# Retention attention with a gated product: where twelve tiles of g are kept, where one product stands, and how the last tile ends

## The chip, the cores and the metric

One NeuronCore of one Trainium2 chip runs the whole program. The metric is the time of one execution on the device in microseconds (us), lower is better. Names of engines: PE is the matrix engine (TensorE), PEld its weight loads, DVE the vector engine, ACT the scalar engine, POOL GpSimd, SP the engine that issues the DMAs (SPq is its queue). A line number with an L is a line of the kernel before, and, in the profile of the kernel after, a line of that one.

## The reference, cut to what matters

Four batches, eight heads, 768 tokens, 64 columns per head. A recurrent attention with one decay per head is followed by a product, a silu and a second product.

```python
gamma = 1.0 - 2.0 ** (-5.0 - np.arange(H))
state = 0
for t in range(S):
    state = gamma * state + k[:, :, t]^T v[:, :, t]        # per batch and head, 64x64
    y[:, :, t] = scale * q[:, :, t] @ state
x = y.transpose(0, 2, 1, 3).reshape(B * S, H * D)           # 3072 x 512
h = x @ w_in                                                # 512 -> 2048
g = h * (1 / (1 + exp(-h)))
return g @ w_out                                            # 2048 -> 512
```

All values are float32, and the kernel computes each product of float32 matrices from parts, so that one product of a tile takes several matmuls.

## The kernel before, in words

**Tiles.** The 768 tokens are cut in six chunks c of 128. A chunk of one batch is a *unit* (c, b), 24 in all, numbered 4c + b. For a unit, PE transposes k and q (the tiles kp, qp; L476 in one form, L485 in a form with 64-row pieces), computes scores within the chunk and the sums for the state (sc, L504 and L514), and y from scores and state (L562). DVE and ACT copy and scale in between (L423, L477, L490, L522, L530, L534, L609), and split x in the parts xt (L633, L636, L639). Such a piece of attention work on PE is called a *visit*. In one form a visit is cut in two halves: the first makes the transposes of unit m and y of unit m − 2, the second the scores of unit m − 1.

**First product.** product_in(c, f) multiplies the four units of chunk c (512 columns of xt) with slice f of 16 of w_in: twelve matmuls of 128x512 (L734), eight into the PSUM tile ha and four into hb. Then close_steps evacuates: ACT copies ha to a tile g (L744), DVE subtracts hb (L749), ACT applies the silu (L754). The tile g lies in the pool hpool, tag "hs", three buffers. put_g stores it to a DRAM tile g_dram[c, f] by a DMA on SP's queue (L757 to L760), one or more products later. (c, f) below means this product.

**Weights.** A slice of w_in is loaded by load_w (three DMAs on SP, L186 and L188), converted (L205 to L224) and split in three parts by split_steps (ACT L121, DVE L124, ACT L127, DVE L129) into a slot of the pool wpool: w0 to w11 and a fourfold slot wq. The slots w4 to w11 hold the k, q and v of the units 0 to 7 first (L161), until those are used up.

**Second product.** For every chunk the g are read back from DRAM (L773), split (L805, L807, L808) and multiplied with w_out: twelve matmuls per (c, f) and four batches into accumulators oa and ob (L1088). In the last chunk the last two slices f are done batch by batch (L1102), and each batch's result is put together and stored: ACT copies ob (L1116), DVE combines with oa (L1121), SP stores (L1124). For the last batch the matmuls into oa go in two halves of 256 columns, and so do the combine and the store.

**Order.** PE's order is written out by hand from end to end. That of SP, DVE, ACT and POOL is by hand only in the head, up to early_order.close() (L976); behind that a scheduler places their instructions, by data and buffers, with hints (issue_after, queue) that put one behind another. The head begins with matmuls on a zero tile (narrow: 128x32, fill: 128x512 and 128x256), which compute nothing that is used; narrow(39), fill(2), narrow(39) stand ahead of the transposes of unit 0 (L858 to L861). Behind the head comes product (1, 0), then, by L980, the first half of visit 10, and then the list steps (L982 to L990): (1,1), (1,2), (0,3), (1,3), (0,4), (1,4), then (0,5), (1,5), (2,0), and so on. Behind each of the first ones the next half visit follows (`behind`, L998). A DMA on SP takes one of eight semaphores in turn, and so waits for the landing of the one eight before.

Of the kernel before, what the change touches and what calls it, by code (L numbers as in the profile page):

```python
# [34 lines left out]
def kernel(  # L35
# [107 lines left out]
    FAR = 3 * B + 2  # L143
    ROWS = range(2 * B + 2, FAR - 1)
    LATER = 4 * B + 2
    early = {}

    def load(name, n):
        if n >= len(units):
# [24 lines left out]
    def load_w(i):  # L174
        if i >= 2 * NF:
            return
        if wide:
            t = stage.tile([128, 2 * DM], U32, tag="wf", name=f"wf_{i}")
            w_in, w_out, n = moe_w_in.bitcast(U32), moe_w_out.bitcast(U32), 256
        else:  # L180
            t = stage.tile([128, DM], FP32, tag="wf", name=f"wf_{i}")
            w_in, w_out, n = moe_w_in, moe_w_out, 128
        if i < NF:
            to = t.rearrange("p (i o f) -> o p i f", o=2, f=n)
            src = w_in[:, ts(i, n)].rearrange("(i o p) f -> o p i f", o=2, p=128)
            nc.sync.dma_start(out=to[0], in_=src[0])  # L186
            for j in range(2):
                nc.sync.dma_start(out=to[1, ts(j, D)], in_=src[1, ts(1 - j, D)])  # L188
        else:
            nc.sync.dma_start(out=t, in_=w_out[ts(i - NF, 128), :])  # L190
        staged[i] = t
# [128 lines left out]
    def narrow(out, n):  # L320

        for _ in range(n):
            nc.tensor.matmul(out[:, :32], lhsT=zero, rhs=zero[:, :32], start=True, stop=True,
                             skip_group_check=True)
# [404 lines left out]
    def multiply(c, f):  # L729
# [6 lines left out]
                                 stop=kk == KIN - 1 and i != 0)  # L736
        return ha, hb

    def close_in(*of):
        list(close_steps(*of))  # L740

    def close_steps(c, f, ha, hb):
        hs = hpool.tile([128, NT], FP32, tag="hs", name=f"g_{c}_{f}")
        copied[:] = [nc.scalar.activation(out=hs, in_=ha, func=AF.Copy, scale=ONE_E).ins]  # L744
        with queue(copied[0]):
            while behind_copy:
                behind_copy.pop(0)()
        yield
        taken_out[:] = [nc.vector.tensor_tensor(out=hs, in0=hs, in1=hb, op=ALU.subtract).ins]  # L749
        with queue(taken_out[0]):  # L750
            while behind_next:
                behind_next.pop(0)()
        yield
        nc.scalar.activation(out=hs, in_=hs, func=AF.Silu)  # L754
        pending.append((c, f, hs))

    def put_g(keep):  # L757
        while len(pending) > keep:
            c, f, g = pending.pop(0)
            stored[:] = [nc.sync.dma_start(out=g_dram[c, f], in_=g).ins]  # L760


    order = [(c, f) for c in range(NC) for f in range(NF)]
# [92 lines left out]
    K, Q = scale_k, scale_q  # L856

    idle[:] = [banks("y", "idle")[:, 0]]  # L858
    narrow(idle[0], 39)
    fill(idle[0], 2)  # L860
    narrow(idle[0], 39)  # L861
    T(0), K(0)
    nc.scalar.activation(out=token, in_=lgc[:1, :1], func=AF.Silu)
    SC(0), A(0), Q(0), A(0), A(0)
# [112 lines left out]
    written[0] = False  # L977

    half_visits = (x for m in range(EARLY + 2, 3 * B + 1) for x in chain(halves(m), (None,)))
    next(half_visits)  # L980

    half = NF // 2  # L982
    pairs = [(1, 1), (1, 2), (0, 3), (1, 3), (0, 4), (1, 4)]
# [12 lines left out]
    takes += [(4, f) for f in (0, 3, 7, 11, 14)]  # L996
    takes += [(5, f) for f in (2, 5, 8)]
    behind = {x: lambda: next(half_visits) for x in pairs[:-1]}  # L998
    behind[pairs[-1]] = lambda: [visit(3 * B + 1), behind_next.append(end_w)]
    at = ([(1, NF - 1)] + [(2, f) for f in range(NF - 7, NF - 2, 2)] +  # L1000
          [(c, 4 * i + 1) for c in range(3, NC - 1) for i in range(B)])
# [17 lines left out]
        turns_at[far[m] + 1], joins_at[far[m] + 3] = m, m  # L1019
    scales_at = {far[m] + 2: m for m in range(LATER - 1, len(units))}  # L1020
    scales_at[steps.index((0, NF - 2))] = FAR
    loads_at = {first_far + 4: [("k", FAR + 1), ("q", FAR + 1)], far[FAR] + 1: [("q", FAR + 2)]}
    for n, (c, f) in enumerate(steps):
        if n in scales_at:
            behind_next.append(lambda m=scales_at[n]: scale_k(m))
        if n in joins_at:
            behind_copy.insert(0, lambda m=joins_at[n]: [join_t(name, m) for name in "qk"])
        if n in parts:
            behind_next.append(lambda m=parts[n]: part_t(m, taken_out[0]))
        patient[0] = steps.index((3, 0)) <= n < max(turns_at) + 2  # L1030
        product_in(c, f)
        put_g(1)
        store_w()
        if (c, f) in takes:
            take_w(taken_out[0], n < len(pairs + three) or c == NC - 1)
        behind.get((c, f), lambda: None)()
        if n in turns_at:
            turn_t(turns_at[n])
            if turns_at[n] >= LATER:
                with tc.issue_after(turned_by[0]):  # L1040
                    load("k", turns_at[n] + 1), load("q", turns_at[n] + 1)
        if turns_at.get(n - 1, 0) >= LATER:
            with tc.issue_after(stored[0]):
                load("v", turns_at[n - 1] + 1)
        if turns_at.get(n - 2, 0) >= LATER:
            with tc.issue_after(stored[0]):
                while waiting:
                    load_w(waiting.pop(0))
        for name, m in loads_at.get(n, ()):
            load(name, m)  # L1050
        if c == NC - 1:
            if f == 0:
                for i in range(W_READ):
                    get_w(i)
            if f < NF - 4:
                w_out(f, True)
            if f >= NF - 6:
                if f == NF - 6:
                    for n in range(G_AHEAD):
                        get(n)  # L1060
                if f >= NF - S_AHEAD:
                    with tc.issue_after(taken_out[0]):
                        split(f - NF + S_AHEAD)
    put_g(0)

    for c in range(NC):
        acc = []
        for b in range(B):
            if b < 2:
                u = banks("sy"[b], f"o{b}_{c}")  # L1070
                acc.append([u[:, i] for i in range(2)])
            else:
                acc.append([turn(f"oa{b}_{c}"), turn(f"ob{b}_{c}") if b == 2 else
                            banks("q", f"ob{b}_{c}", 1)[:, 0]])
        early_f = NF if c < NC - 1 else NF - 2
        for f in range(NF):
            n = c * NF + f
            split(n + S_AHEAD)
            if n < 4:
                w_out(NF - 4 + n)  # L1080
            t = ready[n]
            if f >= early_f:
                continue
            for b in range(B):
                gh, glo, gm = (t[:, i, ts(b, C)] for i in range(3))
                oa, ob = acc[b]
                for o, g, i in (oa, gh, 0), (oa, glo, 1), (ob, gm, 2):
                    nc.tensor.matmul(o, lhsT=g, rhs=wo[f][:, i, :], start=f == 0 and i != 1,  # L1088
                                     stop=f == NF - 1 and i != 0)

        for b in range(B if early_f < NF else 0):
            oa, ob = acc[b]
            ends = [(ob, (2,), slice(None))]
            if b < B - 1:
                ends.append((oa, (0, 1), slice(None)))
            else:
                ends += [(oa, (0, 1), slice(i * DM // 2, (i + 1) * DM // 2))
                         for i in range(2)]
            for o, parts, cols in ends:
                for f in range(early_f, NF):  # L1100
                    for i in parts:
                        nc.tensor.matmul(o[:, cols], lhsT=ready[c * NF + f][:, i, ts(b, C)],  # L1102
                                         rhs=wo[f][:, i, cols], start=False,
                                         stop=f == NF - 1 and i != 0,
                                         skip_group_check=cols.start == DM // 2)
        for b in range(B):
            oa, ob = acc[b]
            o = one.tile([128, DM], FP32, tag=("kt", "qt")[b % 2], name=f"o_{c}_{b}",
                         bufs=(2, 3)[b % 2])
            rows = ds(b * S + c * C, C)  # L1110
            if c < NC - 1:
                nc.scalar.activation(out=o, in_=oa, func=AF.Copy, scale=ONE_E)  # L1112
                nc.vector.tensor_tensor(out=o, in0=o, in1=ob, op=ALU.subtract)
                nc.sync.dma_start(out=out[rows, :], in_=o)
                continue
            nc.scalar.copy(out=o, in_=ob)  # L1116

            n = 2 if b == B - 1 else 1
            for i in range(n):
                cols = ts(i, DM // n)  # L1120
                nc.vector.scalar_tensor_tensor(out=o[:, cols], in0=oa[:, cols], scalar=ONE_E,  # L1121
                                               in1=o[:, cols], op0=ALU.mult,
                                               op1=ALU.subtract)
                nc.sync.dma_start(out=out[rows, cols], in_=o[:, cols])  # L1124


# [28 lines left out]
```

## Time and profile before

| what | value |
|---|---|
| timed runs | 612.46, 613.16, 614.77 us, median 613.16 |
| the profiled execution: its span, first to last instruction | 612.56 us (612.6 on the page) |
| its own time | the span; the median of the timed runs lies 0.6 us above it |
| PE busy in it | 600.9 us, 98% of the span |
| DVE, ACT, POOL busy | 397.1, 324.5 and 32.9 us |
| DMA moved | 108.9 MB, mean 178 GB/s |
| last matmul to the end | 608.8 to 612.6 us |
| granted clock of PE in the page's rows | 1.00 |

How to read it: the page lists busy time per engine, the chain that ended last (followed back from the last instruction, at each step to what released it), and groups of instructions with mean times. Answers of the trace add waits (what ended an engine's idle time), windows (busy time by stretches), and a timeline, where a line has a start in us, a time in us, the engine, the line, the operation with its tiles (out<-in), and in brackets the engine's idle time before it with what ended it. Ends of matmuls are modelled.

### The profile page before, as it was taken

How to read it: one execution, taken by the hardware profiler on the slowest of the kernel's cores; microseconds unless marked ns; L12 is line 12 of the kernel's file. 1: busy time of each engine (PE TensorE's matmuls, PEld its weight loads, DVE VectorE, ACT ScalarE, POOL GpSimd, SP SyncE). 2: the span in 40 equal slices, each digit the busy share in tenths (PEclk: the TensorE clock that was granted, in tenths of full speed). 3: DMA queues.
4: the chain of work that ended last, by engine and by line, in shares of the span. 5: the costliest groups of instructions: out<-in, count | busy, mean ns of one | idle time of the engine just before them, and what ended most of it. 6: DMA issues, size and time to landing. Idle time of an engine off the chain costs nothing.

```text
span 612.6 us, 13713 instructions
## 1 busy us (share of the span) xinstructions
PE 600.9 (98%) x5509; PEld 495.9 (81%) x5509; DVE 397.1 (65%) x672; ACT 324.5 (53%) x598; POOL 32.9 (5%) x89
## 2 busy tenths in 40 slices
PE   8898999999999999999999999999999999999997
PEld 6686788888888888888888888888888888888886
DVE  4797898678886676766689774635545463645631
ACT  7688678678676667676698632212221322313211
POOL 3000020100021111210000000000000000000000
PEclk9999999999999999999999999999999999999999
DMA  9999976586799699998777542623524433433301
GB/s 195 209 199 231 258 214 203 160 254 188 258 231 233 154 263 263 258 291 255 248 249 267 169 138 69 206 69 106 169 72 136 137 110 97 152 123 99 107 1 69
DMA packets 144336, 108.90 MB, mean 178 GB/s; under 512 B 101137, under 2 KB 109585, under 8 KB 144273
## 3 DMA queue, kind: packets, MB, share of 16 engines
q1 hardware_dynamic: 144272, 108.03, 62.3%
q8 instruction: 43, 0.70, 0.5%
q14 instruction: 21, 0.16, 0.1%
HBM read 66.06 MB, written 36.70 MB: 168 GB/s over the span
## 4 chain that ended last, share of the span: by engine, by line
PE 92%; DMA 3%; SPq 2%; DVE 2%; issue 1%; ACT 0%; DVEq 0%
PE ha L734 28%; PE o L1088 21%; PE oa L1088 14%; PE hb L734 14%; PE ob L1088 7%; PE y L562 3%; DMA qf<-in_q_dram 2%; PE sc L504 1%; SPq L166 1%; PE sc L514 1%; DMA kqv<-in_v_dram 1%; SPq L188 1%; PE o L1102 0%; PE oa L1102 0%; PE kp L485 0%
## 5 line engine op out<-in xcount | busy, mean ns | idle before, releaser
L734 PE MATMUL ha<-xt,wi 128*128 128x512 f32 x768 | 193.0, 393 | 0.0
L734 PEld LDWEIGHTS ha<-xt,wi 128*128 128x128 f32 x768 | 142.4, 188 | 30.5 <-DVE xt L636 0.2
L1088 PE MATMUL o<-wo,gs 128*128 128x512 f32 x564 | 143.1, 389 | 0.0
L805 ACT ACTIVATE gs<-gr 128x512 fp32r<-128x512 f32 x96 | 53.2, 621 | 139.0 <-issue 138.0
L1088 PEld LDWEIGHTS o<-wo,gs 128*128 128x128 f32 x564 | 105.9, 188 | 22.0
L807 DVE TENSOR_TENSOR gs<-gr,gs 128x512 fp32r<-128x512 f32 x96 | 62.1, 684 | 94.2 <-ACT gs L805 94.2
L1088 PE MATMUL oa<-wo,gs 128*128 128x512 f32 x376 | 115.7, 389 | 0.0
L749 DVE TENSOR_TENSOR g<-g,hb 128x512 f32<-128x512 f32 x96 | 65.7, 684 | 57.6 <-ACT g L744 42.6
L734 PE MATMUL hb<-xt,wi 128*128 128x512 f32 x384 | 102.7, 389 | 0.0
L734 PEld LDWEIGHTS hb<-xt,wi 128*128 128x128 f32 x384 | 72.1, 188 | 15.1
L1088 PEld LDWEIGHTS oa<-wo,gs 128*128 128x128 f32 x376 | 70.5, 188 | 14.6
L754 ACT ACTIVATE g<-g 128x512 f32<-128x512 f32 x96 | 60.3, 629 | 37.7 <-DVE g L749 37.6
L1088 PE MATMUL ob<-wo,gs 128*128 128x512 f32 x188 | 73.1, 389 | 0.0
L744 ACT ACTIVATE g<-ha 128x512 f32<-128x512 f32 x96 | 56.7, 591 | 28.6 <-PE ha L734 19.8
L808 DVE SCALAR_TENSOR_TENSOR gs<-gs 128x512 fp32r<-128x512 f32 x96 | 62.0, 683 | 0.1
L1088 PEld LDWEIGHTS ob<-wo,gs 128*128 128x128 f32 x188 | 35.3, 188 | 7.4
L205 ACT ACTIVATE ca<-wf 128x512 f32<-128x512 f32 x32 | 21.6, 675 | 6.6 <-DVE cs L218 4.0
L522 DVE TENSOR_TENSOR am<-sc,decay 128x512 f32<-128x512 f32 x24 | 16.5, 687 | 11.4 <-PE sc L514 11.4
L1112 ACT ACTIVATE o<-o 128x512 f32<-128x512 f32 x10 | 6.0, 598 | 33.4 <-PE o L1088 33.0
L218 DVE SCALAR_TENSOR_TENSOR cs<-ca,cs 128x512 uint32<-128x512 uint32 x32 | 22.7, 710 | 0.9
L639 DVE SCALAR_TENSOR_TENSOR xt<-xt 128x512 fp32r<-128x512 f32 x28 | 19.9, 715 | 0.7
L562 PE MATMUL y<-qt,mid 64*64 64x64 f32 x376 | 19.4, 220 | 0.4 <-issue 0.4
(122 smaller groups left out, 562.2 us busy)
## 6 DMA issues: line engine op xcount, KB each, us to landing
gd<-g SPq DMA_DIRECT2D x96, 256.0 KB, 3.7
gr<-gd SPq DMA_DIRECT2D x96, 256.0 KB, 2.7
wf<-in_moe_w_out_dram SPq DMA_DIRECT2D x16, 512.0 KB, 4.7
out_dram<-o SPq DMA_DIRECT2D x23, 256.0 KB, 2.1
wf<-in_moe_w_in_dram SPq DMA_DIRECT2D x16, 256.0 KB, 4.6
wf<-in_moe_w_in_dram SPq DMA_DIRECT2D x32, 128.0 KB, 4.1
kf<-in_k_dram SPq DMA_DIRECT2D x16, 256.0 KB, 4.1
qf<-in_q_dram SPq DMA_DIRECT2D x16, 256.0 KB, 4.1
```

What stands on the lines that cost most here:

```text
L205: top = nc.scalar.activation(out=a.bitcast(FP32), in_=hi.bitcast(FP32), func=AF.Abs, scale=2.0 ** -3).ins
L218: nc.vector.scalar_tensor_tensor(out=s, in0=a, scalar=3, in1=s, op0=ALU.logical_shift_left, op1=ALU.bitwise_xor)
L562: i = nc.tensor.matmul(to[ts(e, D), o, a, :], lhsT=lhsT, rhs=rhs, start=key not in started, stop=True, skip_group_check=True).ins
L639: nc.vector.scalar_tensor_tensor(out=x[2], in0=x[1].bitcast(FP32), scalar=-1.0 / EPS, in1=x[0].bitcast(FP32), op0=ALU.mult, op1=ALU.add)
L734: nc.tensor.matmul(hb if i == 2 else ha, lhsT=w_sb[f][:, i, ts(kk, 128)], rhs=xt[c][:, i, kk, :], start=kk == 0 and i != 1, stop=kk == KIN ...
L744: copied[:] = [nc.scalar.activation(out=hs, in_=ha, func=AF.Copy, scale=ONE_E).ins]
L749: taken_out[:] = [nc.vector.tensor_tensor(out=hs, in0=hs, in1=hb, op=ALU.subtract).ins]
L754: nc.scalar.activation(out=hs, in_=hs, func=AF.Silu)
L805: nc.scalar.activation(out=t[:, 0, :], in_=g, func=AF.Copy, scale=HALF)
L807: nc.vector.tensor_tensor(out=t[:, 1, :], in0=g, in1=high, op=ALU.subtract)
L808: nc.vector.scalar_tensor_tensor(out=t[:, 2, :], in0=t[:, 1, :].bitcast(FP32), scalar=-1.0 / EPS, in1=high, op0=ALU.mult, op1=ALU.add)
L1088: nc.tensor.matmul(o, lhsT=g, rhs=wo[f][:, i, :], start=f == 0 and i != 1, stop=f == NF - 1 and i != 0)
```

## The change

It has four parts. (a) The first twelve tiles g, (0,0) to (0,5) and (1,0) to (1,5), get homes of their own, three each in the slots w7, w9, w10 and w11 of wpool, which are then unused between the k, q, v of units 3, 5, 6 and 7 and the weight slices 7, 9, 10 and 11. Their stores are taken out of the common row and issued later, at the steps that put_later lists, each behind the last load of a weight or the last store (last). (b) The first half of visit 10 no longer stands ahead of (1,1): (1,1) follows (1,0) directly, and behind (1,1) both halves of visit 10 come one after the other. Every other place in PE's order is as it was. (c) The two rows of narrow fillers at the start have 32 and 31 matmuls and not 39 and 39. (d) In the last batch of the last chunk, the last two slices' matmuls for the left half of oa go to a bank of their own, o_left, which starts from nothing. The left half is put together from oa's part (ACT, scaled), ob's (DVE, subtracted) and o_left's (DVE, added); the right half as before. There are still two stores.

```diff
+    early, last = {}, []
...
-            nc.sync.dma_start(out=to[0], in_=src[0])
+            last[:] = [nc.sync.dma_start(out=to[0], in_=src[0]).ins]
...
+    keep_g = {7: [(0, 0), (0, 1), (0, 2)], 9: [(1, 0), (1, 1), (1, 2)],
+              10: [(0, 3), (1, 3), (0, 4)], 11: [(1, 4), (0, 5), (1, 5)]}
+    kept_g = [x for i in keep_g for x in keep_g[i]]
+    homes = {}
+
+    def new_g(c, f):
+        if (c, f) not in kept_g:
+            return hpool.tile([128, NT], FP32, tag="hs", name=f"g_{c}_{f}")
+        i, = (i for i in keep_g if (c, f) in keep_g[i])
+        if i not in homes:
+            homes[i] = wpool.tile([128, 3, NT], FP32, tag=f"w{i}", name=f"gk_{i}")
+        return homes[i][:, keep_g[i].index((c, f))]
...
-        hs = hpool.tile([128, NT], FP32, tag="hs", name=f"g_{c}_{f}")
+        hs = new_g(c, f)
...
-        pending.append((c, f, hs))
-
-    def put_g(keep):
-        while len(pending) > keep:
-            c, f, g = pending.pop(0)
-            stored[:] = [nc.sync.dma_start(out=g_dram[c, f], in_=g).ins]
+        (later if (c, f) in kept_g else pending).append((c, f, hs))
+
+    later = []
+
+    def put_g(keep, of=None):
+        of = pending if of is None else of
+        while len(of) > keep:
+            c, f, g = of.pop(0)
+            with tc.issue_after(last[0]) if of is later else ExitStack():
+                last[:] = stored[:] = [nc.sync.dma_start(out=g_dram[c, f], in_=g).ins]
...
-    narrow(idle[0], 39)
+    narrow(idle[0], 32)
     fill(idle[0], 2)
-    narrow(idle[0], 39)
+    narrow(idle[0], 31)
...
-    next(half_visits)
...
     behind = {x: lambda: next(half_visits) for x in pairs[:-1]}
+    behind[pairs[0]] = lambda: [next(half_visits), next(half_visits)]
...
+    put_later = {6: 1, 7: 2, 9: 1, 10: 1, 11: 1, 13: 1, 14: 1, 15: 1, 16: 1, 17: 2}
...
         put_g(1)
+        if n in put_later:
+            put_g(len(later) - put_later[n], later)
...
-                ends += [(oa, (0, 1), slice(i * DM // 2, (i + 1) * DM // 2))
-                         for i in range(2)]
+                last_left = banks("s", "o_left")[:, 0]
+                ends += [(last_left, (0, 1), slice(0, DM // 2)), (oa, (0, 1), slice(DM // 2, DM))]
...
-            nc.scalar.copy(out=o, in_=ob)
-
-            n = 2 if b == B - 1 else 1
-            for i in range(n):
-                cols = ts(i, DM // n)
-                nc.vector.scalar_tensor_tensor(out=o[:, cols], in0=oa[:, cols], scalar=ONE_E,
-                                               in1=o[:, cols], op0=ALU.mult,
-                                               op1=ALU.subtract)
+            if b < B - 1:
+                nc.scalar.copy(out=o, in_=ob)
+                nc.vector.scalar_tensor_tensor(out=o, in0=oa, scalar=ONE_E, in1=o,
+                                               op0=ALU.mult, op1=ALU.subtract)
+                nc.sync.dma_start(out=out[rows, :], in_=o)
+                continue
+            left, right = (ts(i, DM // 2) for i in range(2))
+            nc.scalar.activation(out=o[:, left], in_=oa[:, left], func=AF.Copy, scale=ONE_E)
+            nc.scalar.copy(out=o[:, right], in_=ob[:, right])
+            nc.vector.tensor_tensor(out=o[:, left], in0=o[:, left], in1=ob[:, left],
+                                    op=ALU.subtract)
+            for x, cols, op in (last_left, left, ALU.add), (oa, right, ALU.subtract):
+                nc.vector.scalar_tensor_tensor(out=o[:, cols], in0=x[:, cols], scalar=ONE_E,
+                                               in1=o[:, cols], op0=ALU.mult, op1=op)
                 nc.sync.dma_start(out=out[rows, cols], in_=o[:, cols])
```

More of the change, by code (lines that the diff above doesn't have):

```diff
@@ L145 @@
     LATER = 4 * B + 2
-    early = {}
+    early, last = {}, []
     def load(name, n):
@@ L1021 @@
     scales_at[steps.index((0, NF - 2))] = FAR
+    put_later = {6: 1, 7: 2, 9: 1, 10: 1, 11: 1, 13: 1, 14: 1, 15: 1, 16: 1, 17: 2}
+    assert sum(put_later.values()) == len(kept_g)
     loads_at = {first_far + 4: [("k", FAR + 1), ("q", FAR + 1)], far[FAR] + 1: [("q", FAR + 2)]}
@@ L1088 @@
                     nc.tensor.matmul(o, lhsT=g, rhs=wo[f][:, i, :], start=f == 0 and i != 1,
-                                     stop=f == NF - 1 and i != 0)
+                                     stop=f == NF - 1 and i != 0 or
+                                     (b, f, i) == (B - 1, early_f - 1, 1))
         for b in range(B if early_f < NF else 0):
@@ L1102 @@
                         nc.tensor.matmul(o[:, cols], lhsT=ready[c * NF + f][:, i, ts(b, C)],
-                                         rhs=wo[f][:, i, cols], start=False,
+                                         rhs=wo[f][:, i, cols],
+                                         start=b == B - 1 and cols.start == 0 and
+                                         (f, i) == (early_f, 0),
                                          stop=f == NF - 1 and i != 0,
-                                         skip_group_check=cols.start == DM // 2)
+                                         skip_group_check=cols.start is not None)
         for b in range(B):
```

## The prediction

> **What bounds it.** I read the engines' busy times first, then the chain that ended last, TensorE's waits, the windows and the timeline.
>
> ```profile
> PE 600.9 (98%) x5509; PEld 495.9 (81%) x5509; DVE 397.1 (65%) x672; ACT 324.5 (53%) x598; POOL 32.9 (5%) x89
> ...
> PE 92%; DMA 3%; SPq 2%; DVE 2%; issue 1%; ACT 0%; DVEq 0%
> ```
>
> TensorE (PE) is busy 98% of the span and is 92% of the chain that ended last. In the chain's rows a product of twelve 128x512 matmuls follows the other by 2.72 us (90.37, 93.09, 95.81): 227 ns a matmul. The change takes away no matmul of a product, so only waits of PE and the end after its last matmul are to be won. PE's waits:
>
> ```profile
> PE sc L504 <- DMA kqv<-in_v_dram: 1.6, 2, 1.1
> PE kp L485 <- DMA qf<-in_q_dram: 1.1, 1, 1.1
> PE idle L323 <- DVE zero L311: 1.0, 1, 1.0
> PE kp L476 <- DMA kqv<-in_k_dram: 0.5, 1, 0.5
> ...
> PE kp L485 <- DMA kf<-in_k_dram: 0.3, 1, 0.3
> ```
>
> The last number is the longest wait. All waits together are some 7 us, and the timeline puts them before 58.6 us; from there to 608.8 I find no gap in PE above 0.06 us. The two that the change can reach are the kp L485 rows, 0.34 and 1.09 us, both in front of visit 10 (unit 10's transposes):
>
> ```profile
> 54.65 1.00 SPq L760 DMA_DIRECT2D gd<-g  x1
> ...
> 55.57 1.08 PE L734 MATMUL hb<-xt,wi 128*128 128x512 f32 x4
> ...
> 56.98 0.24 PE L485 MATMUL kp<-ident,kf 64*128 64x64 f32 x1 [0.34 <-DMA kf<-in_k_dram]
> ...
> 58.54 0.27 PE L485 MATMUL kp<-ident,qf 64*128 64x64 f32 x1 [1.09 <-DMA qf<-in_q_dram]
> ...
> 59.79 2.11 PE L734 MATMUL ha<-xt,wi 128*128 128x512 f32 x8
> ...
> 62.74 0.69 PE L504 MATMUL sc<-vf,kf 64*64 64x64 f32 x32
> ```
>
> Columns: start, time, engine, line, operation, in brackets PE's idle time before it and what ended it. Product (1,0) ends with the four matmuls from 55.57. PE then waits for kf and qf of unit 10, does the first half of visit 10, and only at 59.79 starts (1,1), whose operands have long been there. At 62.74 the second half follows, and (1,2) starts at 64.06. Both loads were issued behind stores on SP's queue (50.46 for 0.54 us, 54.65 for 1.00).
>
> **Part 1, (1,1) behind (1,0): −1.8 us.** (1,0)'s last four matmuls start at 55.57 and take 4 x 0.227, so (1,1) can start at 56.47. Its slice of w_in and xt are there, and the banks it writes were emptied by ACT (the evacuation of (1,0) ends at 56.54, and the pair used before that is free). A product up to the step behind it takes 2.95 (59.79 to 62.74; 72.78 to 75.73 again), a first half without a wait 1.50 (67.01 to 68.51), a second half 1.32 (62.74 to 64.06). So (1,2) starts at 56.47 + 2.95 + 1.50 + 1.32 = 62.24, not 64.06: −1.8. Visit 10's transposes come at 59.42, after qf's landing at 58.49. Bounds: −1.4 if only the two waits go, −2.0 if the second half, now right behind the first, saves its own start too. The second half uses unit 9's tiles, copied and scaled by 56.13, so it waits for nothing of the first.
>
> Is the gain kept to the end? From 64 us PE's releasers were ready before PE by at least 0.49 us (DVE's evacuation ahead of 95.64), at 68.5 and 93.8 by 0.56 to 0.60, elsewhere by 0.78 or more. DVE is the nearest:
>
> ```profile
> 60.00:70.00 10.00, 10.00 (x174) 8.00 (x174) 6.62 (x12) 6.94 (x16) 2.33 (x4) 1.00 1.03 255
> 70.00:80.00 10.00, 10.00 (x175) 7.91 (x173) 9.16 (x16) 7.50 (x16) 1.31 (x3) 1.00 0.84 234
> 80.00:90.00 10.00, 10.00 (x242) 8.52 (x241) 9.43 (x17) 7.42 (x14) 2.25 (x3) 1.00 0.84 229
> 90.00:100.00 10.00, 10.00 (x46) 8.29 (x45) 9.31 (x18) 7.69 (x15) 0.00 (x0) 1.00 0.60 192
> ```
>
> Columns: stretch, its length, busy PE, weight loads, DVE, ACT and POOL, granted clock (1.00), DMA share, GB/s. DVE is 92 to 94% busy from 70 to 100, but it had 3.4 of 10 us free from 60 to 70, and its dense stretch begins with am L522 of unit 9, which PE's scores at 63.9 release. If PE comes 1.8 us earlier, so does DVE's stretch. I keep the full 1.8.
>
> **Part 2, the kept g: 0 us.** Twelve stores of 256 KB leave SP's queue between 38 and 96 us and come back between about 88 and 122 us, behind a weight load or another store. In the old places (0,0) and (0,1) held SP 0.85 us at 38.13 and 0.54 at 50.46 ahead of unit 10's loads, and each moved 256 KB, 1.1 us at the 235 GB/s of the stretch 50 to 60. Without them qf of unit 10 lands some 2 us earlier (about 56.3). That would remove by itself the wait that part 1 already removes: the two don't add. The 0.26 us that PE waited for qf of unit 9 at 52.73 gives nothing either, since (1,0)'s second group waits for xt (DVE L636, 54.48) with 0.1 us to spare.
>
> The added waits: the first writes of the slots w7, w9, w10 and w11 (ACT L121, at 98.81, 110.82, 120.52 and 126.11) now wait until the slot's three stores have landed. Behind that ACT instruction stand L212, L754 and the next evacuations L744, for which PE waits; PE has about 1.8 us to spare there. By the step that issues them and the 3.7 us to landing in the table of DMA issues, I estimate the slots free some 3 us ahead of the first three writes and 0.5 to 1 us ahead of w11's. On SP's queue the stores now stand ahead of weight loads (96.27 to 119.65) and of the transposed loads at 116.83 and 118.29; the weight loads feed conversions some 5 us later (96.27 to ACT L205 at 102.27), which belongs to rival B, while the transposed tiles are used far later, near 170. In exchange ACT no longer waits for a buffer's store at 67.35 and 88.55. Below nothing it can't go, as PE waits for nothing there; above, see rival B. I take 0.
>
> **Part 3, 15 narrow fillers fewer: 0 us.** They are 7 of the first 39 (1.23 us, 27 ns each as they pass) and 8 of the second (1.25): 0.4 to 0.5 us less before the first transposes.
>
> ```profile
> 2.87 1.25 PE L323 MATMUL idle<-zero 128*128 128x32 bf16 x39
> ...
> 4.25 0.80 PE L476 MATMUL kp<-ident,kqv 128*128 128x128 f32 x4
> ...
> 5.33 0.66 PE L476 MATMUL qp<-ident,kqv 128*128 128x128 f32 x4
> ...
> 6.54 0.69 PE L504 MATMUL sc<-kqv 64*64 64x64 f32 x32 [0.45 <-DMA kqv<-in_v_dram]
> ```
>
> The fillers end at 4.12 and k of unit 0 lands at 4.11, so at most 0.1 us is won there. What hides it are the next waits, for q (0.35) and v (0.45). The first kp takes 0.80 and the later ones 0.65 or less: PE becomes faster within it, though the granted clock in the rows reads 1.00. [...]
>
> [...]
>
> **Part 4, the last left half in its own bank: +0.7 us.**
>
> ```profile
> 607.67 1.11 PE L1102 MATMUL oa<-wo,gs 128*128 128x256 f32 x8
> 607.87 0.59 ACT L1116 COPY o<-ob 128x512 f32<-128x512 f32 x1 [0.74 <-PE ob L1102]
> 608.88 0.76 DVE L1121 SCALAR_TENSOR_TENSOR o<-oa,o 128x256 f32<-128x256 f32 x2 [0.71 <-PE oa L1102]
> ```
>
> Before, ACT copies ob beside the last eight matmuls, and after the last one DVE does two combines of 256 columns; the left one, complete after four matmuls, also starts only after the eighth. Their stores leave at about 609.33 and 609.76, and the span ends at 612.56, 2.8 us behind the second. After, the left half needs four instructions: ACT L1147 scales oa's left half, DVE L1149 subtracts ob's, then come DVE's two combines L1152. In the built program ACT does the right copy L1148 first, and L1147 waits for PE's last matmul, because the right half's matmuls write the same bank; DVE has L1149 first, so the right combine stands behind it. So after 608.88: ACT 0.37 (256 columns from PSUM, L490), DVE 0.34, 0.34 and 0.41 (256-column pitch and end of L530 and L534), hops of about 0.1. The last store leaves at 610.4 to 610.5, not 609.76: +0.7. Bounds: +0.3, if the left subtract runs beside PE (the order of the end doesn't hold), +1.0 with hops as long as the longest here.
>
> **Sum.** 612.56 − 1.8 + 0 + 0 + 0.7 = 611.5 against the profiled span of 612.56. That execution's span is 0.6 below the median of 613.16 (612.46 to 614.77), so I put the sum on the median's scale: **612.1**.
>
> **Rivals.**
> - **A, the gain is given back (13%): 613.9.** DVE at 93% from 70 to 100 is the next bound: if its order there makes the 0.49 us at 95.6 negative, PE waits again and 1.8 is lost, while the tail's 0.7 stays. Against it: DVE's idle 3.4 us at 60 to 70.
> - **B, the kept slots come free late (12%): 614.5, slower than before.** Place: ACT L121 of w10 and w11. Twelve stores are 3.1 MB, 12.6 us at 250 GB/s; from 90 to 122 DMA is 0.51 to 0.60 busy, which leaves some 14 us. If the free share is a tenth smaller than that, the stores end 3 us late, ACT waits, and after PE's 1.8 us are used up the rest is PE's: 1.2 us at each of two slots, +2.4. For it: the stretch 120 to 130 is already at 0.89 and ACT there waited 0.42 for a store.
> - **C, the tail does as the code reads (10%): 610.8 to 611.** The left half is ready before PE's last matmul, and DVE then has one combine less to do after it: −0.4 in place of +0.7. Against it: L1147's wait.
> [...]
>
> **Chances.** Forecast 60%, with its own range 611.2 to 613.0, A 13, B 12, C 10, D 5. The range takes in A, C and most of B's lower half: 610.6 to 614.4. About 0.5% (3 us) is what a measurement of this kernel can tell from no change: faster than 610.1 needs C with the highest gain of part 1, 0.04; slower than 616.2 needs B with a third slot, 0.03; within, 0.93.
>
> **What would show it.** Part 1: (1,1) starts at about 56.5 and (1,2) at 62.2, no bracket ahead of kp L485, and a constant 1.8 us between the two kernels' products from there to the end. Part 2: no ACT L121 with a wait for gd<-g above 1 us; PE without a gap from 88 to 130. Part 3: kp of unit 0 at about 4.25 still, sc of unit 0 at 6.54. Part 4: the last store 1.6 us behind PE's last matmul, not 1.0. The forecast is wrong if PE has new gaps after 62 us or if the left combine starts ahead of PE's end.

## The result, and the profile after

| | before | after |
|---|---|---|
| median of 13 runs each, side by side | 612.46 us (611.56 to 617.07) | 617.46 us (614.81 to 620.20) |
| ratio, with its 95% interval | 1 | 1.0065 (1.0043 to 1.0087) |
| span of the profiled execution | 612.6 us | 615.6 us |

The change made the kernel slower by some 4 to 5 us (4.0 by the ratio, 5.0 by the medians), where 612.1 was forecast, about 1 us below the median of before. In all runs after, the time is 1.8 us above the span, and in the runs of before that lie beside the experiments 1.7 to 1.9. A span of 612.6 thus belongs to a time of 614.4, one of the three longest of the thirteen: the profiled execution of before was not a typical one. The traces differ by 3.1 us, and this is where, by the start of the same product of PE in both:

```
product        before   after   after - before
(0,0) first     27.52   28.54   +1.02
second          36.79   37.87   +1.08
third           42.60   43.67   +1.06
(1,0)           53.44   55.60   +2.16
(1,1)           59.79   58.55   -1.24
(1,2)           64.06   64.03   -0.03
... constant from here to
the 39th       163.64  163.61   -0.03
the 41st       171.20  172.07   +0.87
the 42nd       174.06  176.45   +2.39
... constant to the last matmul
last matmul    608.78  611.17   +2.39
end of span    612.56  615.63   +3.07
```

So there are four steps up and one down: +1.06 in the head, +1.1 at 52, −2.2 by the new place of (1,1), +2.4 at 166 to 176, +0.7 at the end. The waits of PE after:

```profile
PE kp L476 <- DMA vf<-in_v_dram: 1.9, 1, 1.9
PE sc L504 <- issue: 1.5, 2, 0.9
...
PE ha L734 <- DVE xt L636: 0.7, 1, 0.7
PE kp L476 <- POOL step L368: 0.6, 1, 0.6
...
PE ha L734 <- ACT xt L633: 0.3, 1, 0.3
PE hb L734 <- DVE xt L639: 0.3, 1, 0.3
```

The two kp L485 rows of before are gone, as forecast. In their place stand a wait of 1.9 us that is put down to a load of v, waits for "issue" (nothing that the profile shows), and three waits for the parts xt. The timeline of PE in the head, after:

```profile
2.68 1.03 PE L323 MATMUL idle<-zero 128*128 128x32 bf16 x31
4.28 1.09 PE L476 MATMUL kp<-ident,kqv 128*128 128x128 f32 x4 [0.56 <-POOL step L368]
5.15 0.42 PE L323 MATMUL idle<-zero 128*128 128x32 bf16 x8
5.41 1.09 PE L476 MATMUL qp<-ident,kqv 128*128 128x128 f32 x4
6.30 0.34 PE L323 MATMUL idle<-zero 128*128 128x32 bf16 x5
6.63 1.13 PE L504 MATMUL sc<-kqv 64*64 64x64 f32 x32
```

The fillers end 0.56 us before the transposes, and kp, qp and sc take 1.09, 1.09 and 1.13 us where before they took 0.80, 0.66 and 0.69. The record of the granted clock begins with full speed at 10.28 us here, and at 4.62 before (the pages of the profile read 1.00, since nothing is recorded ahead of that). At 52 us, after:

```profile
54.42 0.66 PE L476 MATMUL kp<-ident,kf 128*128 128x128 f32 x4 [1.89 <-DMA vf<-in_v_dram]
```

The named load is not what kp needs: it reads kf of unit 9, which landed at 47.36, seven us earlier. In the same gap the queue q8 carries code; the DMA part for 51.8 to 54.4 us:

```profile
q1 hardware_dynamic: 1962, 0.49, 94.3%
q8 instruction: 1, 0.02, 3.2%
```

That packet is 16 KB, starts at 51.83 and takes 1.35 us; PE resumes 1.24 us after its end. At 166 to 176, and at the end:

```profile
172.07 1.20 PE L734 MATMUL ha<-xt,wi 128*128 128x512 f32 x4 [0.34 <-ACT xt L633]
173.92 1.19 PE L734 MATMUL ha<-xt,wi 128*128 128x512 f32 x4 [0.66 <-DVE xt L636]
175.46 1.15 PE L734 MATMUL hb<-xt,wi 128*128 128x512 f32 x4 [0.34 <-DVE xt L639]
```

```profile
610.53 0.64 PE L1124 MATMUL oa<-wo,gs 128*128 128x256 f32 x4
611.21 0.38 ACT L1147 ACTIVATE o<-oa 128x256 f32<-128x256 f32 x1 [0.58 <-PE oa L1124]
611.62 0.42 DVE L1149 TENSOR_TENSOR o<-o,ob 128x256 f32<-128x256 f32 x1 [1.07 <-DMA out_dram<-o]
611.96 0.42 DVE L1152 SCALAR_TENSOR_TENSOR o<-oa,o 128x256 f32<-128x256 f32 x1
612.30 0.42 DVE L1152 SCALAR_TENSOR_TENSOR o<-o_left,o 128x256 f32<-128x256 f32 x1
```

ACT's scaling starts only after PE's last matmul, and three instructions of DVE follow it in a row.

### The profile page after: what moved, and what is told of

It is laid out like the page before. It is cut to its first block, busy times and chain, and to the rows that moved or that the text cites. A ratio compares the mean times of both kernels' runs of the same rounds, so it can differ in the third digit from the quotient of the medians.

```text
span 615.6 us, 13680 instructions
## 1 busy us (share of the span) xinstructions
PE 602.5 (98%) x5494; PEld 497.0 (81%) x5494; DVE 396.8 (64%) x673; ACT 324.6 (53%) x599; POOL 34.1 (6%) x89
## 4 chain that ended last, share of the span: by engine, by line
PE 91%; DMA 4%; DVE 1%; SPq 1%; issue 1%; ACT 1%; DVEq 0%
PE ha L734 27%; PE o L1109 21%; PE oa L1109 14%; PE hb L734 13%; PE ob L1109 7%; PE y L562 4%; PE sc L504 2%; PE sc L514 2%; DMA kqv<-in_v_dram 1%; DMA yr<-yd 1%; DMA wod<-cw 1%; SPq L166 1%; PE kp L476 1%; DMA vf<-in_v_dram 1%; PE qp L476 0%
## 5 line engine op out<-in xcount | busy, mean ns | idle before, releaser
L762 DVE TENSOR_TENSOR g<-g,hb 128x512 f32<-128x512 f32 x84 | 57.5, 685 | 52.7 <-ACT g L757 41.5
L767 ACT ACTIVATE g<-g 128x512 f32<-128x512 f32 x84 | 52.7, 628 | 30.9 <-DVE g L762 30.1
L757 ACT ACTIVATE g<-ha 128x512 f32<-128x512 f32 x84 | 49.8, 593 | 25.2 <-PE ha L734 17.8
L1137 DVE TENSOR_TENSOR o<-o,o 128x512 f32<-128x512 f32 x10 | 6.8, 688 | 19.3 <-ACT o L1136 19.3
```

## The experiments

The theory after the result (**T**): the cut fillers cost twice, by the clock (C) and by the places at which PE's code ends its blocks of 256 instructions (P; the expectations call such a block a page); the kept g cost by what the later stores do to the order of DVE and ACT (O); (1,1) gains; the end loses. The rivals stand in the expectations. Each kernel was timed against before on the same chip, 11 or 12 runs against 17 to 35.

**Fillers back to 39 and 39, the rest of the change kept.**

```diff
-    narrow(idle[0], 32)
+    narrow(idle[0], 39)
     fill(idle[0], 2)
-    narrow(idle[0], 31)
+    narrow(idle[0], 39)
```

> The changed kernel with the two rows of narrow fillers at 39 and 39 again, all else of the change kept. Theory T (the fillers decide when the clock is released, and with their 30 instructions where PE's pages of instructions end): clock at full from 4.6 us and not from 10.3, the products up to 47 us 1.06 us earlier than in the changed kernel and level with before, no gap of 1.9 us in PE at 52.5, then what remains of the change: at most -1.4 to -2.2 at 56 to 64, +2.4 at 166 to 176, +0.65 at the end, so 2 to 2.5 us faster than the changed kernel and 1 to 2 slower than before. Rival R1 (the late release and the gap are chance of one execution): median level with the changed kernel, +5 us on before.

616.05 against 614.11, ratio 1.0027 (0.9996 to 1.0057). Full clock from 4.80; products 1.03 earlier than before up to 47 us (T had them level: before itself stops 1.12 us at 17.73, this kernel doesn't), so 2.06 earlier than after; the gap at 52 is 0.94 us, halved and not gone; 0.45 us of a wait for DVE's evacuation at 164.78 and 0.34 of one for xt at 172.41; 4.46 us from PE's last matmul to the end. That is near what T has, and it speaks against R1. But the interval takes in 1, so the medians don't show that what remains is slower than before.

**Only the fillers cut**, the same two lines the other way round, on the kernel before.

> The kernel before with only the fillers cut to 32 and 31. [...] Rival R1: the same as before within 0.5 us, and a clock at full from 4.6 us.

616.93 against 614.11, 1.0037 (1.0007 to 1.0066): slower by 2.3 in the ratio, as T has it, and not within 0.5 us as R1 has it. The clock was at full from 4.75 in the profiled execution, so the late release does not come in each one; the first 47 us lost only 0.5. But PE stopped twice near 50, with its data there:

```profile
50.35 0.64 PE L562 MATMUL y<-am,kqv 64*64 64x64 f32 x29 [1.22 <-ACT qt L477]
54.27 0.65 PE L476 MATMUL kp<-ident,kf 128*128 128x128 f32 x4 [1.82 <-issue]
```

Counted in PE's records (weight loads, matmuls and the few semaphore instructions, in order of start; a few records are missing), the two gaps stand ahead of the 2241st and the 2498th. In after, the gaps at 18.80, 23.59, 49.96 and 54.42 stand ahead of the 705th, 962nd, 2241st and 2498th; in before those at 17.73, 22.20 and 27.06 ahead of the 707th, 961st and 1217th. All are 193 to 195 more than a multiple of 256. PE's code comes in blocks of 16,384 bytes on queue q8 (43 packets in before and in after), and PE stops where a block ends and the next is not there. The list of waits of before had such stops already, put down to "issue" (22.20 and 27.06):

```profile
PE qp L476 <- issue: 0.4, 1, 0.4
PE y L562 <- issue: 0.4, 1, 0.4
```

The two stops near 50 aren't the whole loss. Where they stand, the waits for unit 10 go, so at (1,2) this trace is only 0.20 us behind before. It ends 5.2 us behind: 1.3 come at 172 to 176 (more on this below, behind the start with 28 instructions fewer), and 2.8 at 289 to 306, where PE waits for ACT's evacuations (0.53 and 1.66).

Of the 43 blocks of after, PE stops ahead of four (waits of 0.24 to 1.89 us), as where it runs 256 instructions in 2.6 us (49.96 to 52.54) and goes on with the next block only at 54.42, 4.5 us after it began the last. Ahead of the others its trace has no such wait above 0.2 us.

**Only (1,1) behind (1,0).**

```diff
-    next(half_visits)
...
+    behind[pairs[0]] = lambda: [next(half_visits), next(half_visits)]
```

> The kernel before with only (1,1) put behind (1,0). Theory T: no waits ahead of the transposes of unit 10, (1,2) starts 1.4 to 2.0 us earlier, kept to the end: 1.4 to 2.0 faster where the waits are in the executions at all, -0.5 to -2 in the medians. Rival A of the prediction (given back at 70 to 100): level with before, with new gaps in PE at 92 to 96.

613.66 against 614.11, 0.9994 (0.9969 to 1.0020). In the trace (1,2) starts 2.26 us earlier than before, and this stays to the end (last matmul 606.56, not 608.78), with no new gap behind it: rival A falls. Of the 2.26, 1.1 are there from the first products on, ahead of the move (26.45 beside 27.52), because before stops at 17.73 and this kernel doesn't; about 1.15 belong to the move. In the medians it is not to be told from nothing; here the block's end at 51.65 cost 1.46 us, and in before it cost nothing. While PE stops there, the loads of unit 10 catch up, so the wait that is removed is smaller or not there (none is left with the cut alone, which stops for 1.82 us at 54.27).

**Only the kept g.** The definitions of keep_g, new_g and put_later on the kernel before.

> The kernel before with only the kept g and their later stores. Theory T: the order of DVE and ACT from 133 to 171 us comes out otherwise and the late x (read of y back, xt) comes late: PE gaps at 166 to 176 of 1.5 to 2.4 us together, against the waits at 56 to 58 that go because the loads of unit 10 are earlier (-1.4): +0.5 to +1.5 on before. Rival B of the prediction: ACT's first writes of w10 and w11 wait for stores by over 1 us and PE gaps stand at 120 to 130. Rival R2: nothing at 166 to 176, and -1.4.

616.07 against 614.11, 1.0032 (1.0003 to 1.0060): slower by about 2. Some 0.35 of it lies outside the span: here the times are 2.1 to 2.2 us above their spans, in all other kernels 1.7 to 1.9. Between product (1,2) and the 42nd it loses 1.8 us, of it 0.20 and 0.34 as gaps at 166 and 174, the rest in shorter waits. ACT never waited for a store at the first writes of the slots (in after it was 0.2 us in all): rival B of the prediction falls. From 139 to 173 us DVE's order is another than in before.

**Short start, blocks as before**: 32 and 31 fillers, and 15 more behind q's transposes of unit 0.

```diff
-    NARROW_T = {0: (8, 5)}
+    NARROW_T = {0: (8, 20)}
```

> The kernel before with the two rows of fillers cut to 32 and 31 as in the change, and 15 narrow fillers more behind the transposes of q of unit 0 (20 and not 5), where PE waits for v. So PE's later instructions lie where they lay before, and only the start is shorter. Theory P (the cut costs because PE's pages of 256 instructions then end elsewhere: gaps of 1 to 2 us at two page ends, 49 and 52.5, and not at one): level with before, 613.5 +-0.5 at full clock. Theory C (it costs because the clock is released later): as with the cut alone, +2 to +3 us on before.

616.66 against 614.75, 1.0032 (1.0011 to 1.0053). No gap at either block's end near 50; but the fillers ended at 3.71 and the transposes came at 4.28, and the clock was full from 9.58, half again from 12.99, full from 16.41. The first product comes 1.56 late. So the clock costs too, as C has it. But the run doesn't hold C without P: PE stopped at block ends at 12.50 (1.05) and 23.89 (0.72), and the half speed from 12.99 follows the first of these. Of the 3.6 us by which this trace is longer than that of before, 1.4 stand at (1,2); most of the rest comes from 190 us on, with waits for ACT's evacuations at 206.99 (0.39) and 303.76 (0.53).

**Long start, blocks moved**: 15 fillers taken out behind the start.

```diff
-    NARROW_T = {0: (8, 5)}
+    NARROW_T = {0: (0, 0)}
...
-    NARROW_Y = {0: 8}
+    NARROW_Y = {0: 6}
```

> The kernel before with the two rows of 39 as they were, and 15 narrow fillers taken away behind them (13 at the transposes of unit 0, 2 ahead of its y), where PE waits for DMA or DVE anyway. So the clock's start is untouched and every later instruction of PE lies 30 places earlier, as in the change. Theory P: page ends as with the cut alone, with gaps at the scores of unit 8 and the transposes of unit 9 (some 49 and 52), +2 to +3 us on before at full clock. Theory C: level with before.

616.15 against 614.75, 1.0017 (0.9996 to 1.0039): not certain in the medians. In the trace the clock is full from 4.84, and the gaps ahead of the 2242nd and 2497th record are 0.99 and 2.62 us; (1,0) is 2.2 us late as in after, and the waits for unit 10 take in most of it: (1,2) is 0.33 late. Another 1.26 are lost at 172 to 176, the same as with the cut alone.

**Slots only**: the kept g in their slots, stored in the common row.

```diff
-        (later if (c, f) in kept_g else pending).append((c, f, hs))
+        pending.append((c, f, hs))
...
-    put_later = {6: 1, 7: 2, 9: 1, 10: 1, 11: 1, 13: 1, 14: 1, 15: 1, 16: 1, 17: 2}
+    put_later = {}
```

> The kernel before with the twelve g in slots of their own, but stored in the common row as before: the order on every engine is that of before. Theory L (part 1 of the cost of the kept g is the later stores: DMA and the order of DVE and ACT that follows from them): level with before, no gap in PE at 164 to 176 beyond those of before. Theory S (it is the slots: their first writes wait): +2 us on before, with the wait at the first writes of w7 to w11.

615.36 against 614.75, 1.0015 (0.9992 to 1.0038), and no gap after 52 us. So no cost of the slots can be told.

**The right half in its own bank**, on (1,1) behind (1,0).

```diff
+                last_right = banks("s", "o_right")[:, 0]
+                ends += [(oa, (0, 1), slice(0, DM // 2)), (last_right, (0, 1), slice(DM // 2, DM))]
...
+                if n == 2 and i == 1:
+                    nc.vector.scalar_tensor_tensor(out=o[:, cols], in0=last_right[:, cols],
+                                                   scalar=ONE_E, in1=o[:, cols],
+                                                   op0=ALU.mult, op1=ALU.add)
```

> The kernel before with (1,1) behind (1,0), and at the end the other half in a bank of its own: the last two slices' matmuls for the left half go into oa as before, those for the right half into a new bank. DVE then combines both halves with oa while PE works on the right half, and after PE's last matmul only one combine of 256 columns is left. Theory B (a bank is the unit that a wait guards): the last store leaves about 0.6 us after PE's last matmul and not 1.0, from PE's last matmul to the end 3.4 us and not 3.78 (before) or 4.46 (the change); in the medians 0.3 to 0.4 below (1,1) behind (1,0) alone, so -0.5 to -1 on before. Rival: the store's 2.8 us to the end of the span takes the place, no difference.

614.52 against 614.75, 0.9994 (0.9972 to 1.0016); from PE's last matmul to the end 3.91 us. Theory B's gain did not come: DVE did start before PE's end, as theory B says, but ACT's copy of ob, which ends at 609.61, now came last ahead of it, and three combines in a row from there end no earlier than two from PE's last matmul.

```profile
609.02 0.59 ACT L1119 COPY o<-ob 128x512 f32<-128x512 f32 x1 [0.74 <-PE ob L1103]
609.17 0.55 PEld L1103 LDWEIGHTS o_right<-wo,gs 128*128 128x128 f32 x4
609.29 0.64 PE L1103 MATMUL o_right<-wo,gs 128*128 128x256 f32 x4
609.64 0.76 DVE L1124 SCALAR_TENSOR_TENSOR o<-oa,o 128x256 f32<-128x256 f32 x2 [0.32 <-ACT o L1119]
```

**As long a start, 28 instructions fewer.**

```diff
-    narrow(idle[0], 39)
-    fill(idle[0], 2)
-    narrow(idle[0], 39)
+    narrow(idle[0], 32)
+    fill(idle[0], 3)
+    narrow(idle[0], 31)
```

> The kernel before with the fillers at the start as 32 narrow, 3 wide, 31 narrow: as long a start as before (a wide one of 128x512 takes about as long as 15 narrow ones), but 28 instructions of PE fewer, so its pages of 256 end nearly where the change puts them. Theory P (pages): the gaps at the y of unit 6 (49) and at the transposes of unit 9 (52) as in the cut alone, +1 to +2 us on before. Theory C (clock): PE without a gap ahead of its first transposes, full clock from 3.9 to 7 us, level with before.

617.65 against 614.34, 1.0050 (1.0018 to 1.0082), with full clock from 3.70 and transposes at 4.15. P's gaps are there (0.67 and 2.29), and C alone would have it level. It is more than P said: the clock was at half again from 13.94 to 17.36, behind a wait of 1.6 us for q of unit 1.

```profile
51.27 0.69 PE L562 MATMUL y<-am,kqv 64*64 64x64 f32 x32 [0.67 <-ACT qt L477]
55.70 0.27 PE L562 MATMUL y<-qt,mid 64*64 64x64 f32 x1 [2.29 <-issue]
```

This kernel, the cut alone and the long start with moved blocks lose once more at one place: 1.25 us between the 41st and the 42nd product. In all three DVE and ACT run in the very order of before, yet the second y that is read back there lands 6.4 to 6.6 us after its issue, against 4.2 to 4.7 in the ten kernels whose blocks don't lie 28 or 30 places earlier. ACT in before, then ACT and PE with the cut alone:

```profile
168.21 0.62 ACT L633 ACTIVATE xt<-yr 128x512 fp32r<-128x512 f32 x1
```

```profile
171.11 0.63 ACT L633 ACTIVATE xt<-yr 128x512 fp32r<-128x512 f32 x1 [1.72 <-DMA yr<-yd]
175.01 1.17 PE L734 MATMUL hb<-xt,wi 128*128 128x512 f32 x4 [0.94 <-DVE xt L639]
```

In the three a packet of PE's code starts at 168.0 to 169.6, while that y is on its way, and in after too (167.80; that y takes 5.7 us). In the ten others none does. No run moves that packet alone, so that it is what delays y rests on this coincidence.

**Kept g, stored at the steps 5 to 15.**

```diff
-    put_later = {6: 1, 7: 2, 9: 1, 10: 1, 11: 1, 13: 1, 14: 1, 15: 1, 16: 1, 17: 2}
+    put_later = {5: 1, 6: 1, 7: 1, 8: 1, 9: 1, 10: 1, 11: 1, 12: 1, 13: 1, 14: 1, 15: 2}
```

> The kernel before with the twelve g kept and stored later, but at the steps 5 to 15 and not 6 to 17: DVE and ACT then have the very order of before, and only SP's order differs. Theory O (the cost of the kept g is the other order of DVE and ACT from 133 to 171 us, which makes the late x late): level with before or up to 1 us faster, no gap in PE from 164 to 176. Theory D (it is the stores themselves, on the DMA and on SP's queue between 88 and 122): +1.5 to +2.5 us, as with the kept g alone.

614.14 against 614.34, 0.9993 (0.9969 to 1.0018): the 2 us are gone, with twelve stores still moved. PE has no gap from 53 to 200 us. DVE and ACT run in the order of before, as theory O asks. The steps also move the stores on SP's queue, and no run changes the one without the other; the rows speak for the order of DVE and ACT. DVE at 155 to 163 with the kept g alone, and then with these steps:

```profile
155.88 0.68 DVE L762 TENSOR_TENSOR g<-g,hb 128x512 f32<-128x512 f32 x1
156.48 0.68 DVE L224 CUSTOM_DVE_ANT_0 cw<-wf,cs 128x1024 uint16<-128x1024 uint16 x1
...
162.43 0.69 DVE L224 CUSTOM_DVE_ANT_0 cw<-wf,cs 128x1024 uint16<-128x1024 uint16 x1 [1.10 <-DMA wod<-cw]
163.04 1.29 DVE L636 TENSOR_TENSOR xt<-yr,xt 128x512 fp32r<-128x512 f32 x2
```

```profile
153.98 0.69 DVE L224 CUSTOM_DVE_ANT_0 cw<-wf,cs 128x1024 uint16<-128x1024 uint16 x1
154.59 0.68 DVE L761 TENSOR_TENSOR g<-g,hb 128x512 f32<-128x512 f32 x1
...
159.93 0.69 DVE L224 CUSTOM_DVE_ANT_0 cw<-wf,cs 128x1024 uint16<-128x1024 uint16 x1 [0.66 <-DMA wod<-cw]
160.54 0.68 DVE L761 TENSOR_TENSOR g<-g,hb 128x512 f32<-128x512 f32 x1
161.13 1.29 DVE L636 TENSOR_TENSOR xt<-yr,xt 128x512 fp32r<-128x512 f32 x2
```

In the first the conversion of a weight, cw (L224), stands behind the evacuation of g, in the second ahead of it. Its store is issued later, the next cw waits for that store to land, and behind that cw in DVE's order stand the parts xt, which free the buffer for the next y to be read back. By xt the first is 1.9 us behind the second (0.7 of it is the distance of the two traces, by the 39th product), and PE waits for what is made of that y.

**Blocks moved by 98 records, and the end once more**: seven wide fillers each as eight narrow ones, ob of the last batch one place earlier, on the kernel with the right half's own bank.

```diff
-    FILL_T = {2: (3, 2), 3: (0, 1)}
+    FILL_T = {2: (24, 16), 3: (0, 8)}
...
-                fill(tp[i], FILL_T.get(n, (0, 0))[i])
+                narrow(tp[i], FILL_T.get(n, (0, 0))[i])
...
-    FILL_Y = {0: 1, 3: 4}
-    NARROW_Y = {0: 8}
+    FILL_Y = {3: 4}
+    NARROW_Y = {0: 16}
...
+            ends.insert(len(ends) - (b == B - 1), (b, ob, (2,), slice(None)))
```

> (1,1) behind (1,0), the right half in its own bank as before, ob of the last batch one place earlier in PE's order, and seven wide fillers (of units 0, 2 and 3) each replaced by eight narrow ones of the same length, so that PE's later instructions lie 98 places further on and its pages end elsewhere. Theory P: the gap at the page end near 52 us goes, and the pages near 41 to 50 us come without a gap above 1 us; with the row of last stores 0.4 us earlier, 1 to 2 us faster than before at full clock. Theory C: the pages don't matter, -0.4 to -0.9.

618.26 against 614.34, 1.0052 (1.0027 to 1.0077): slower, where both theories had it faster. The gaps between 35 and 55 us did go (none at a block's end above 0.21), but others end at 188.77 (0.27) and 195.64 (0.94), ahead of the 5570th and 5825th record, again 194 and 193 more than a multiple of 256. The end took 4.37 us, because oa of the batch before came later and three combines of DVE queued. It also loses 1.9 us between (1,2) and 139 us, and 1.2 between 196 and 304; I did not find why. After 200 us PE waits for ACT's evacuations in six of the fourteen traces (0.34 to 1.66 us each), this one among them, and that stays open too.

**What is left of the change**: fillers as before, end as before, (1,1) behind (1,0), kept g stored at the steps 5 to 15.

> The change without what the runs so far found to cost: fillers 39 and 39, the end of before, the kept g with the steps 5 to 15, and (1,1) behind (1,0). DVE and ACT in the order of before but for the one move at (1,1). If the four parts' costs are what the other runs say (order of DVE and ACT, page ends and clock, the end): no gap in PE between 53 and 300 us, the end at 3.8 us after PE's last matmul, 0.5 to 1.5 us faster than before in the medians. If there is another cost in the kept g that the earlier steps only hid: level with before or slower.

612.46 against 613.86, 0.9976 (0.9952 to 1.0000): about 1.4 us faster, at the edge of what can be told. PE's last matmul is at 607.19, and after 50 us the trace has one gap, 0.35 at 298. It has the lowest median of the kernels; it wasn't timed side by side with after.

## Why the prediction was wrong, step by step

- **The base** failed first: the sum was put on the median by adding 0.6 us to the profiled span. It is 1.8 us; the profiled execution was one of the longest of before, and one with the full wait for unit 10. That is 1.2 us of the distance, and not the step that turned a gain into a loss.
- **Part 1**, −1.8 us. The mechanism was right, and nothing was given back at 70 to 100, as argued. The last experiment, without a stop near 50 us, wins 2.1 us between the third product and (1,2). After and the move alone win 1.1 and 1.15 over the same stretch, since they stop for code within it. But the term was sized from one execution; over the runs (1,1) alone gave −0.4, within its interval of nothing.
- **Part 2**, 0 us, failed: +2 (kept g alone). "Below nothing it can't go, as PE waits for nothing there; above, see rival B" looked for a price at the first writes of the slots only. The slots and the stores cost nothing that can be told (615.36 and 614.14 beside 614.75 and 614.34); the price lay 40 us later, where the later stores had come with another order of DVE and ACT. The prediction doesn't name that order, nor the chain cw, store, cw, xt that hangs on it, in which DVE already waited in before (0.45 us for wod<-cw at 161.01). The kept g alone lose 1.4 us at 166 to 176. After loses 2.4 there; the 1 us between the two is what the moved blocks could have added, by the late y above.
- **Part 3**, 0 us, failed: +2.3 to 2.8 (fillers cut alone). "What hides it are the next waits" counted the fillers as time only. They are also what keeps PE busy ahead of the transposes (idle there for 0.56 us in after, 0.13 in before), and 30 instructions whose absence moves every later end of a block. Near 50 us the two gaps at block ends sum to 2.1, 3.0, 3.6 and 3.0 us in the four traces with blocks 28 or 30 places earlier, and to 0 to 2.1, mean 0.9, in the nine with blocks as in before. The waits for unit 10 take in most of that, and the late y at 172 to 176 adds 1.25 in three of the four. The 5% for D in the chances stand for a PE that stays slow for longer at the start, an estimate of the author's that no trace of before shows; in after full clock comes at 10.28 us, in before at 4.62. The head of after is 1.06 behind that of before, and 2.06 behind that of the same kernel with 39 and 39, so the waits behind it did not hide it.
- **Part 4**, +0.7 us: right, 4.46 against 3.78 from PE's last matmul to the end, in the order that was read from the built program. Two traces show it (after, and the one with 39 and 39 fillers); it wasn't timed alone.

By medians the parts done alone sum to −0.4 + 2.0 + 2.8 + 0.7 = +5.1, and the change measured +5.0. The intervals of the first three are 1.5 to 1.8 us wide to each side, and the parts act on the same waits, so that the two agree this well is luck.

How part 3 splits between clock and blocks can be told in part from the granted clock that is listed with every timed run. It reads 0.997 and 0.996 in the two profiled runs that went back to half speed for 3.4 us (the short start with blocks as before, the start with 28 instructions fewer), and 0.998 to 1.000 in the others; a late first release doesn't enter it (0.999 for after). Among the runs at 0.998 or more, the cut alone has a median of 615.61 (7 runs) beside 613.51 for before (20), and the moved blocks alone 616.15 (5) beside 614.18 (19): +2.1 and +2.0. So without later half speed, moving the blocks costs about what the cut costs, with the start untouched. What the clock adds isn't settled: with the short start and blocks as before all 11 runs read 0.997 or less (16 of 35 in before beside it), with the cut alone only 5 of 12 (15 of 35).

## What to carry to other kernels

Before a sum is made from one profiled execution, see where its time lies among the runs; a wait that is long in it may be short in most. An instruction that does nothing still holds a place: here 15 fillers fewer at the start moved every later block end by 30 places, and the moved blocks alone cost some 2 us. So in code dense with small matmuls it pays to look for gaps whose record numbers are equal modulo the block. When a scheduler places an engine's work, compare its order over the whole program, and follow each swapped pair to the next store and load that hang on it. Where runs scatter, compare those with the same granted clock: here that turned "not certain" (1.0017, 0.9996 to 1.0039) into +2.0 us, if of 5 runs beside 19.

## What the runs showed of the hardware

- PE's code arrives in blocks of 16 KB, each taking 0.9 to 2.5 us on the queue. At the stops near 50 us, 3.2 to 6.1 us passed from a block's start to the next one's being there, with the DMA share at 0.67 or more. PE resumed 1.2 to 1.8 us after the fetch had ended. The waits list gives such gaps to "issue", or to whatever load or copy landed near them.
- Full clock begins at 3.70 to 6.91 us in the eleven traces with a full start and in one of the three with a cut one (4.75); in the other two at 9.58 and 10.28. Where it changed more than once the changes lie 3.41 us apart (9.58, 12.99, 16.41). Half speed reads 0.50 in the record (before's from 612.19 us on, after's from 614.44). In the two traces that went back to half speed, PE's gaps in the 3.41 us ahead of it sum to 1.11 and 1.87 us; in six others 1.1 to 1.7 us of gaps in such a stretch weren't followed by it, and what decides it stays open.
